# What the planner of a TensorE-bound kernel counts: instruction fetches, and the SBUF turns of VectorE and GpSimd

## The chip, the cores and the metric

The kernel runs on one core of one Trainium2 chip. The core has five engines that run in parallel, each through its own list of instructions: TensorE (matrix products, PE in the profile, with its weight loads as PEld), VectorE (DVE), ScalarE (ACT), GpSimd (POOL) and SyncE (SP), which issues every DMA of this kernel. [...] The metric is the time of one execution on the device in microseconds (us); lower is better. The median of three runs stands for a kernel.

## The reference

Two computations, one after the other. First a chunked attention: 4 batches of 8 heads, 768 tokens, 64 values per head; every chunk of 32 queries sees 16 tokens to its left, itself, 8 to its right, and 8 memory tokens, so 64 keys. Then a mixture of 8 experts over all 3072 tokens of width 512, with a gate that is balanced by eight rounds of row and column division:

```python
scores = scale * np.matmul(q_c, k_full.transpose(0, 1, 3, 2))
a = np.exp(scores - np.max(scores, axis=-1, keepdims=True))
a = a / (np.sum(a, axis=-1, keepdims=True) + 1e-09)
out[:, :, c_start:c_end] = np.matmul(a, v_full)
...
P = np.exp(logits - logits.max())
for _ in range(8):
    P /= P.sum(1, keepdims=True) + 1e-09
    P /= P.sum(0, keepdims=True) + 1e-09
    P *= N / E
for e in range(E):
    h = np.maximum(x @ w1[e], 0.0)
    out += P[:, e:e + 1] * (h @ w2[e])
```

All of it is float32.

## The kernel before

**The work.** The tokens are cut into six units of 512 tokens. With 8 experts that makes 48 pairs of an expert and a unit, handled in one long sequence. A float32 product is made of float16 products: each operand is split into a high and a low half, and three passes (high by high, and the two mixed ones) are added up in PSUM (`PASSES`, L1625). The products of a unit are made by a scheme with seven block products in place of eight (`P1` to `P7`), so sums and differences of blocks are formed first, by VectorE and GpSimd, and split too. A product task on TensorE (`product`, L1629) is 6 or 12 matmuls of 256 columns; the first expert's second layer (`plain_output`, L2138) has tasks of 6 matmuls of 512 columns.

**The attention** is done in 24 blocks of 128 queries (`transposed`, `scores`, `values`), between the products of the first five units. A block has four short tasks of four 128x128 transposes (`tq`, `tk`, `tx`, `ta`) and two bursts: the scores (`sp`, L1103) and the weighted values (`xp`, L1181), each of 64 small matmuls, every one with a weight load of its own. For each unit of 512 tokens come 32 small matmuls of the gate (`lp`, L1437). The results are turned, scaled and split into the unit's operand `x` (`build`, L1283), part of which VectorE and GpSimd form (`sums`, L1314). While a bank of PSUM is free and TensorE would wait, `Plan.pad` (L128) puts matmuls on nothing there (`warm`, L428); this stops when the attention's buffers are given back (`turn`, L2253, at the fifth unit).

**The order of work.** The whole kernel is first written down as some thousands of tasks, and `Plan.run` (L139) then puts them into an order by simulating the engines: each task has an engine, a cost in us, a priority (a due time), the tasks that it depends on, and perhaps a PSUM bank that it takes or frees. At each step the task that can start first is issued; among those that can start at once on an engine, the one with the lowest priority value. Only this order goes to the chip: the instructions of an engine are emitted in it, and the framework adds the semaphore waits that the data need. The costs and the simulated times have no other effect. DMA tasks follow a simple model of one pipe (`pipe`, L143): a transfer starts behind those before it, and the issuer may run up to `BEHIND` = 5 us ahead.

Details that matter here:

- The products of one sequence are chained (`last_pe`, L1646), so among themselves they stay in one order; what the planner decides on TensorE is where attention tasks, the gate, small reductions and `plain_output` go between them.
- Tasks that read PSUM or free something urgently have a priority 200 us ahead of time (`FIRM`).
- In the steady stage (from the fifth unit on, `LATE`) a unit is 28 product tasks of the first layer and 14 of the second; VectorE does, among others, `c` (L1695, one input from PSUM), `ss` (L1794), `h` (L1838 and L1854), `acc` (L1969, L2003); GpSimd does `acc` (L1959), and the sums of blocks of the weights (`ws`, L620).
- `first_hidden` (L2049) makes the first layer of the first unit in two groups g of 256 tokens, each in two steps k. Its tokens come from `xops[0][0]`, apart from g = 1, k = 0, whose tokens lie in a corner of another buffer (`room`, L2058). `xops[0][1]` is the list of the four splits that make them, in the order (g, k) = (0,0), (0,1), (1,1), (1,0) (`build`, L1371 to L1380). The task for (g, k) depends on entry 2g + k (L2085).
- `burst` and `quiet` (L163, L196) could keep two bursts apart by `APART`, which is 0.

## Time and profile before

| what | us |
|---|---|
| median of 3 runs | 1923.76 (1922.41 to 1924.03) |
| the profiled execution, its own time | 1923.72 |
| its span, first to last instruction | 1921.9 |
| TensorE busy in the span | 1893.2 |
| VectorE, ScalarE, GpSimd busy | 1461.6, 1026.7, 545.8 |

The profile is one execution. It lists groups of instructions by line, engine and tile, who waited for whom, the chain of work that ended last, the busy time of each engine in any stretch, and the DMA queues. A matmul row counts matmuls; each has a weight load beside it, listed as PEld. "Busy" of TensorE is not the same as fast: the profile also lists the clock that TensorE was granted (PEclk). "Issue" is waiting for which the profile shows no other engine or transfer as the cause.

### The profile page before, as it was taken

Reading aid. Unit: us, or ns where it says so; the run is one execution under the profiler, and the core shown is the slowest. Engines: PE = TensorE matmul, PEld = TensorE weight load, DVE = VectorE, ACT = ScalarE, POOL = GpSimd, SP = SyncE. Lnnn points to the kernel's source line nnn. Section 1 sums busy time; section 2 is a strip of 40 time slices with the busy share of each in tenths; the row PEclk is TensorE's granted clock in tenths of the full one; section 3 lists DMA queues with packets and bytes.
Section 4 is the critical chain, followed back from the end, with each engine's and each line's share of the span. In section 5 each row is a group of like instructions: output and inputs, shape, how many; then the busy total and the mean of one; then the engine's idle time right before and its main releaser. Section 6 shows DMA issues by size and latency. Waiting matters only on the chain.

```text
span 1921.9 us, 46741 instructions
## 1 busy us (share of the span) xinstructions
PE 1893.2 (99%) x19467; PEld 1628.2 (85%) x19467; DVE 1461.6 (76%) x2417; ACT 1026.7 (53%) x2008; POOL 545.8 (28%) x576
## 2 busy tenths in 40 slices
PE   8899999999999999999999999999999999999999
PEld 7666676688888888888888888888888888888888
DVE  5876879778679866898668875898678885786565
ACT  6665554656456545646445554655555564564453
POOL 2421102434223321442124231342124232332112
PEclk9999999999999999999999999999999999999999
DMA  9866863453234342255215433244413632322321
GB/s 214 205 131 148 222 178 120 135 180 136 84 121 160 127 145 87 89 192 180 91 62 171 175 105 127 89 159 163 140 45 122 222 124 91 102 84 83 127 83 67
DMA packets 209100, 253.98 MB, mean 132 GB/s; under 512 B 108792, under 2 KB 142584, under 8 KB 204536
## 3 DMA queue, kind: packets, MB, share of 16 engines
q1 hardware_dynamic: 208888, 251.00, 41.8%
q8 instruction: 152, 2.49, 0.5%
q14 instruction: 60, 0.49, 0.1%
HBM read 187.51 MB, written 63.44 MB: 131 GB/s over the span
## 4 chain that ended last, share of the span: by engine, by line
PE 92%; DVE 5%; DMA 1%; issue 1%; ACT 1%; SPq 0%; POOL 0%; DVEq 0%; POOLq 0%; ACTq 0%
PE px L1636 25%; PE yx L1636 23%; PE pz L1636 12%; PE yz L1636 11%; PE py L1636 6%; PE yy L1636 6%; PE yp L2154 4%; DVE ss L1794 1%; PE xp L1181 1%; PE pp L2073 1%; PE sp L1103 1%; DVE x L523 1%; PE warm L428 1%; PE ta L1170 1%; PE tq L1040 0%
## 5 line engine op out<-in xcount | busy, mean ns | idle before, releaser
L1636 PEld LDWEIGHTS <-w 128*128 128x128 f16 x7896 | 771.3, 98 | 99.0 <-issue 8.0
L1636 PEld LDWEIGHTS <-h 128*128 128x128 f16 x7056 | 690.4, 98 | 80.9 <-issue 1.1
L1636 PE MATMUL px<-x,w 128*128 128x256 f16 x4512 | 549.6, 273 | 5.5 <-DVE c L1695 3.4
L1959 POOL TENSOR_TENSOR acc<-acc,y 128x256 f32<-128x256 f32 x252 | 269.5, 1076 | 881.7 <-ACT y L1934 868.4
L1636 PE MATMUL yx<-w,h 128*128 128x256 f16 x4032 | 467.5, 273 | 0.7 <-ACT y L1934 0.7
L1685 ACT ACTIVATE q<-px 128x256 f32<-128x256 f32 x376 | 143.1, 382 | 299.2 <-PE px L1636 295.1
L1636 PE MATMUL pz<-x,w 128*128 128x256 f16 x2256 | 278.2, 273 | 0.7 <-DVE c L1695 0.7
L1636 PE MATMUL yz<-w,h 128*128 128x256 f16 x2016 | 233.8, 273 | 0.0
L1854 DVE TENSOR_TENSOR h<-ss,h 128x1024 f16<-128x1024 f32 x160 | 208.6, 1305 | 3.9 <-ACT h L1830 3.7
L1805 ACT ACTIVATE h<-c 128x768 f16<-128x768 f32 x168 | 140.8, 838 | 110.4 <-DVE c L1695 110.4
L1830 ACT CAST h<-ss 128x1024 f16<-128x1024 f32 x168 | 174.2, 1039 | 30.2 <-DVE ss L1794 30.1
L1838 DVE SCALAR_TENSOR_TENSOR h<-c,h 128x768 f16<-128x768 f32 x168 | 167.5, 997 | 12.8 <-ACT h L1805 12.5
L1794 DVE SCALAR_TENSOR_TENSOR ss<-c,ss 128x256 f32<-128x256 f32 x336 | 168.7, 502 | 8.1
L1695 DVE SCALAR_TENSOR_TENSOR c<-px,q 128x256 f32<-128x256 f32 x188 | 78.6, 421 | 107.0 <-PE px L1636 101.6
L1636 PE MATMUL py<-x,w 128*128 128x256 f16 x1128 | 139.5, 273 | 0.0
L1934 ACT ACTIVATE y<-yx,pscale 128x256 f32<-128x256 f32 x168 | 79.4, 474 | 112.5 <-PE yx L1636 108.5
L2154 PE MATMUL yp<-w,h 128*128 128x512 f16 x576 | 131.1, 379 | 0.1
L1794 DVE SCALAR_TENSOR_TENSOR ss<-c,h 128x512 f32<-128x512 f32 x168 | 125.9, 749 | 2.5 <-ACT h L1782 2.5
L1695 DVE SCALAR_TENSOR_TENSOR c<-py,q 128x256 f32<-128x256 f32 x188 | 78.8, 422 | 60.3 <-PE py L1636 54.5
L1636 PE MATMUL yy<-w,h 128*128 128x256 f16 x1008 | 116.9, 273 | 0.0
L2154 PEld LDWEIGHTS <-h 128*128 128x128 f16 x576 | 55.1, 98 | 61.9 <-issue 1.8
L515 ACT ACTIVATE w<-ws,sw 128x1024 f16<-128x1024 f32 (+1 forms) x64 | 69.5, 1088 | 60.5 <-POOL ws L620 60.5
(168 smaller groups left out, 1783.2 us busy)
## 6 DMA issues: line engine op xcount, KB each, us to landing
x<-xkeep SPq DMA_DIRECT2D x28, 1792.0 KB
akeep<-acc SPq DMA_DIRECT2D x168, 256.0 KB
acc<-akeep SPq DMA_DIRECT2D x168, 256.0 KB
w1f<-in_moe_w_dram SPq DMA_DIRECT2D x36, 512.0 KB
w2f<-in_moe_w_dram SPq DMA_DIRECT2D x32, 512.0 KB
w1fm<-in_moe_w_dram SPq DMA_DIRECT2D x28, 512.0 KB
w2fm<-in_moe_w_dram SPq DMA_DIRECT2D x28, 512.0 KB
xkeep<-x SPq DMA_DIRECT2D x6, 1792.0 KB
```

The lines of the kernel that those rows point to most:

```text
L515: lambda: nc.scalar.activation(dst(0), src(), AF.Copy, scale=s),
L1636: nc.tensor.matmul(dst.t, a, b, start=(not more and n == 0), stop=(n == end), skip_group_check=more,)
L1685: lambda: nc.scalar.activation(t.t, src.t, AF.Copy, scale=DOWN),
L1695: lambda: nc.vector.scalar_tensor_tensor(c.t[:, o], src.t, DOWN, q.t, op0=ALU.mult, op1=ALU.add),
L1794: lambda: nc.vector.scalar_tensor_tensor(dst(), src(), 0.0, other(), op0=ALU.max, op1=op),
L1805: lambda: nc.scalar.activation(h.t[:, 0, 0:3], c.t, AF.Relu),
L1830: lambda: nc.scalar.copy(h.t[:, 0, 3:7], ss.t),
L1838: lambda: nc.vector.scalar_tensor_tensor(h.t[:, 1, 0:3].rearrange("p a n -> p (a n)"), c.t.rearrange("p a n -> p (a n)"), 0.0, h.t[:, 0, 0 ...
L1854: lambda: spare.tensor_tensor(h.t[:, 1, 3:7], ss.t, h.t[:, 0, 3:7], op=ALU.subtract),
L1934: (lambda: nc.scalar.activation(t.t, src.t, AF.Copy, scale=f))
L1959: lambda: nc.gpsimd.tensor_tensor(acc.t[:, cols], acc.t[:, cols], q.t, op=ALU.add),
L2154: nc.tensor.matmul(py.t, hf.t[:, hl, where[fh], o : o + P], room(fp, WIDE * wl + DM * fh, WIDE * wl + DM * (fh + 1)), start=(fp == 0 and i ...
```

## The change

The planner's model gets two more things, and many costs in it are corrected. No instruction is added to the kernel or taken out of it, apart from the number of padding matmuls, which `pad` works out from the simulated gaps; the instructions come in another order.

**Fetches.** Every TensorE task gets a `size`, its number of instructions (two per matmul: weight load and product; two passes for a float32 one). `count` adds them up. Whenever the count passes 161 + 256k, a fetch is noted, taken to land 1.4 us later plus 0.8 of the backlog of the DMA pipe, at most 6 us; instructions behind number 449 + 256k can't start before it has landed. `earliest` gives the time at which a task can start so that it doesn't run into a fetch that hasn't landed, and `run` uses it as one more condition of the start. `burst`, `quiet` and `late` are gone.

**Turns on SBUF.** Tasks of GpSimd (but the partition reduction) and those of VectorE that are marked `port=True` are simulated as taking turns: such a task starts no earlier than 0.3 us before the end of the other engine's last one. Their costs become those of the operation by itself (GpSimd's 128x256 operation 0.74 in place of 0.9 or 0.95, and so on).

**One dependency.** The task for (g, k) in `first_hidden` depends on entry 3g + k - 2gk, that is 0, 1, 3, 2 for (0,0), (0,1), (1,0), (1,1).

```diff
-APART = 0.0
+BLOCK = 256
+ASKS = 161
+HELD = 288
+FETCH = 1.4
+QUEUED = 6.0
+FREE = 0.3
...
+        t.size = size
+        t.port = eng == "POOL" if port is None else port
...
                     self.fill(bank, n)
                     heappush(banks, (now + 0.11 * n + 0.2, bank))
+                    self.count(2 * n, now, 0.11 * n)
...
+    def count(self, size, at, cost):
+        while self.counted + size > self.asks:
+            when = at + cost * (self.asks - self.counted) / size
+            queued = min(0.8 * max(self.pipe - when, 0.0), QUEUED)
+            self.fetches.append((self.asks + HELD, when + FETCH + queued))
+            self.asks += BLOCK
+        self.counted += size
+        self.fetches = [f for f in self.fetches if f[1] > at + cost]
+
+    def earliest(self, t, at):
+        for end, landed in self.fetches:
+            if t.size and self.counted + t.size > end:
+                at = max(at, landed - t.cost * (end - self.counted) / t.size)
+        return at
...
-                        if t.burst and at < quiet:
-                            late = (at, t, a) if late is None else late
-                            continue
+                        at = self.earliest(t, at)
                         if pick is None or at < pick[0]:
                             pick = (at, t, a)
...
             t.start = at
-            if t.burst:
-                quiet = at + APART
+            if t.size:
+                self.count(t.size, at, t.cost)
+            if t.port:
+                at = max(at, self.held["POOL" if t.eng == "DVE" else "DVE"] - FREE)
+                self.held[t.eng] = at + t.cost
...
-            sums.append(add("POOL", 0.95, tt(*op), [ld] + sums[-1:], prio - 5, [st, ws]))
+            sums.append(add("POOL", 0.74, tt(*op), [ld] + sums[-1:], prio - 5, [st, ws]))
...
             takes=sp,
-            burst=True,
+            size=4 * H * CB,
...
-        t = add("PE", 0.9, go, [t] + lv, at + 2, [vt, aT], takes=xp, burst=True)
+        t = add("PE", 0.9, go, [t] + lv, at + 2, [vt, aT], takes=xp, size=4 * H * CB)
...
-        t = add("PE", cost, go, list(deps) + [last_pe[0]], now[0], bufs, takes=takes)
+        t = add("PE", cost, go, list(deps) + [last_pe[0]], now[0], bufs, takes=takes, size=int(24 * cost / STEP / 2))
...
             "POOL" if aside else "DVE",
-            2.3 if aside else 1.23,
+            2.15 if aside else 1.23,
             lambda: spare.tensor_tensor(h.t[:, 1, 3:7], ss.t, h.t[:, 0, 3:7], op=ALU.subtract),
             [shi],
             at - 1.0,
             [h, ss],
+            port=True,
...
-                    [t, *wmade, xops[0][1][2 * g + k]],
+                    [t, *wmade, xops[0][1][3 * g + k - 2 * g * k]],
```

## The prediction, made before the result was known

> **What bounds the kernel now.** I read the page first, then the busy time by stages, who TensorE waited for after the first 50 us, and the chain of work that ended last.

> ```profile
> span 1921.9 us, 46741 instructions
> ...
> PE 1893.2 (99%) x19467; PEld 1628.2 (85%) x19467; DVE 1461.6 (76%) x2417; ACT 1026.7 (53%) x2008; POOL 545.8 (28%) x576
> ...
> q8 instruction: 152, 2.49, 0.5%
> ```

> ```profile
> 0.00:50.00 50.00, 43.47 (x789) 35.24 (x790) 30.38 (x63) 31.04 (x63) 14.06 (x25) 0.97 0.98 210
> 50.00:355.00 305.00, 292.17 (x4521) 207.69 (x4519) 240.88 (x447) 169.99 (x342) 66.51 (x77) 0.99 0.65 164
> 355.00:420.00 65.00, 61.26 (x464) 45.11 (x462) 51.98 (x67) 32.98 (x61) 35.24 (x32) 1.00 0.51 171
> 420.00:1900.00 1480.00, 1477.52 (x13530) 1323.56 (x13529) 1133.98 (x1834) 789.85 (x1538) 425.62 (x436) 1.00 0.36 121
> ```

> TensorE is the bound: busy in 1893.2 of 1921.9 us. The second fence is the busy time by stages (columns: length, then PE, PEld, DVE, ACT, POOL; the granted clock; DMA share; GB/s). From 420 to 1900 us TensorE is idle for 1480 - 1477.52 = 2.48 us at full clock: three quarters of the kernel have almost nothing to give. The idle time is in the attention: 305 - 292.17 = 12.83 us from 50 to 355, 3.74 in the next 65, and 6.53 in the first 50, where the DMA share is 0.98.

> ```profile
> PE sp L1103 <- issue: 5.2, 3, 2.2
> PE px L1636 <- ACT q L1685: 2.1, 2, 1.7
> ...
> PE lp L1437 <- issue: 1.5, 1, 1.5
> ```

> ```profile
> 21.96 2.47 issue
> ...
> 44.43 7.00 DMA k<-in_k_dram
> ...
> 86.01 2.23 issue
> ...
> 121.37 1.60 issue
> ...
> 168.36 1.33 issue
> ...
> 237.66 1.52 issue
> ```

> Half of the 12.83 us is put down to nothing ("issue"): three waits in the score bursts and one in the gate's. All four stand in the chain that ended last (start, length, what), so each delays the end: 2.23 + 1.60 + 1.33 + 1.52 = **6.68 us**. A fifth, 2.47, comes before 50 us, and behind it the chain runs through a 7.00 us DMA.

> **What the four are.** The same table by stages, cut at these stalls, counts the matmuls between them:

> ```profile
> 32.00:88.20 56.20, 49.17 (x1014) 36.97 (x1014) 46.82 (x76) 40.09 (x80) 18.34 (x18) 1.00 0.93 219
> 88.20:122.95 34.75, 31.58 (x507) 21.75 (x506) 27.77 (x46) 20.36 (x42) 11.80 (x16) 0.95 0.64 146
> 122.95:169.65 46.70, 44.58 (x759) 31.14 (x760) 32.35 (x56) 26.03 (x52) 6.42 (x9) 1.00 0.61 131
> 169.65:239.10 69.45, 67.74 (x1264) 47.89 (x1264) 53.61 (x89) 35.55 (x76) 7.16 (x9) 1.00 0.80 192
> ```

> With a weight load each they are 2028, 1014, 1518 and 2528 instructions, just short of 8, 4, 6 and 10 blocks of 256 (2048, 1024, 1536, 2560). The page's queue for instructions moved 2.49 MB in 152 packets, and 2 x 19467 / 152 = 256. So TensorE runs out of instructions at a block's boundary, when the next block is late. Why it is late, the DMA queues show, from 81.05 to 87.0 us:

> ```profile
> q1 hardware_dynamic: 705, 2.18, 94.6%
> q8 instruction: 1, 0.02, 1.0%
> ```

> and the busy time in the five us before the stall:

> ```profile
> 81.05:86.00 4.95, 4.92 (x146) 4.01 (x144) 4.57 (x9) 3.78 (x9) 0.00 (x0) 1.00 0.98 383
> ```

> The DMA engines are full there (0.98), and one block's packet is among 706. Meanwhile 146 matmuls, 292 instructions, went by: two bursts and short tasks. The same number in products of six matmuls in 0.66 us would take 16 us. A block is late where bursts follow each other while the queue is full.

> **The change part by part.**

> *The fetch model.* `earliest` holds back a burst that would run into a block still on its way; a task of 12 instructions goes first. That costs nothing where such a task is ready, and behind each of the four stalls one was run at once. The most to be had is 6.68 us and one clock loss:

> ```profile
> 88.20:92.80 4.60, 4.55 (x41) 3.24 (x48) 1.98 (x3) 1.76 (x4) 1.37 (x3) 0.63 0.43 94
> ```

> ```profile
> 89.06 1.49 PE L2073 MATMUL pp<-x,w 128*128 128x256 f16 x6
> ...
> 92.72 0.89 PE L1181 MATMUL xp<-v_pair,at 64*32 64x65 f32 x64
> 93.54 0.83 PE L2073 MATMUL pp<-w,w 128*128 128x256 f16 x6
> ...
> 95.52 0.82 PE L2073 MATMUL pp<-x,w 128*128 128x256 f16 x6
> ```

> After the 2.23 us stall the granted clock was 0.63 for 4.6 us. Three tasks of six matmuls took from 89.06 to 92.72, 3.66 us; the next three took from 93.54 to 95.52, 1.98. That is 1.68 us more, so 8.36 in all. After the three shorter stalls the clock stayed at 1.00. [...]

> Against it stands how the planner counts. Between the stalls 20, 10, 18 and 32 instructions are missing to whole blocks: TensorE issues things that are no matmul and no weight load (waits, it seems), and `size` has no term for them. The planner's boundary then lies behind the real one by at least 20, 30, 48 and 80 instructions at the four stalls, up to a third of a block. The early two should be foreseen; for the later two, I take half. Bounds: all 8.36, or the first stall alone (2.23 + 1.68 = 3.91).

> *What is late next.* A burst held back gives its scores later, and VectorE's work behind them. The nearest row for a product that waits for VectorE in this stage is the first here:

> ```profile
> 137.25 0.81 PE L1636 MATMUL pz<-x,w 128*128 128x256 f16 x6 [0.73 <-DVE c L1695]
> ...
> 842.77 0.82 PE L1636 MATMUL px<-x,w 128*128 128x256 f16 x6 [0.62 <-DVE c L1695]
> ...
> 1505.35 0.81 PE L1636 MATMUL px<-x,w 128*128 128x256 f16 x6 [0.62 <-DVE c L1695]
> ```

> I take one such wait, +0.73; bounds 0 and two.

> *The first 50 us.* A stall of 2.47 could go, but the DMA share there is 0.98 and the planner has little but padding to run meanwhile. I take 0; bounds 0 and -2.47.

> *Turns on SBUF.* The rows bear the rule out:

> ```profile
> 363.76 2.89 POOL L1854 TENSOR_TENSOR h<-ss,h 128x1024 f16<-128x1024 f32 x1 [2.64 <-ACT h L1830]
> 364.60 2.61 DVE L1794 SCALAR_TENSOR_TENSOR ss<-c,h 128x512 f32<-128x512 f32 x1
> ...
> 407.62 0.68 DVE L1794 SCALAR_TENSOR_TENSOR ss<-c,h 128x512 f32<-128x512 f32 x1
> ...
> 1903.12 0.73 POOL L1959 TENSOR_TENSOR acc<-acc,y 128x256 f32<-128x256 f32 x1 [8.68 <-DMA acc<-akeep]
> ```

> VectorE's sum takes 0.68 us alone and 2.61 when GpSimd has begun (364.60 + 2.61 = 367.21, just 0.56 behind GpSimd's end at 366.65). GpSimd's 0.73 agrees with the new 0.74. On the chip nothing changes but the order: simulated VectorE becomes later, so other tasks are ready when it picks. What it can win are the waits for VectorE and ScalarE after 355 us, 3.74 + 2.48 = 6.22; products keep their order there, and VectorE is busy 1133.98 of 1480, so it has room. What it can lose is the last rival. The sign is open; I take 0, bounds -6.22 and +9.9 (below). SyncE issues the same DMAs in an order that follows the tasks; at a DMA share of 0.36 to 0.65 after 50 us I take nothing for it.

> *The dependency.*

> ```profile
> 62.08 1.21 DVE L523 SCALAR_TENSOR_TENSOR w<-xg,sx,w 128x512 f16<-128x512 f32 x1
> ...
> 70.59 0.82 PE L2073 MATMUL pp<-w,w 128*128 128x256 f16 x6
> ```

> The tokens in the corner are ready at 63.29, and the first product that reads them starts at 70.59 without a wait: seven us of cover, so 0. Without the cover it would cost one split, 1.21.

> **The sum.** Profiled execution 1923.72 (span 1921.9 and 1.8 around it; the median, 1923.76, is 0.04 more): -2.23 - 1.68 - 1.60 for the early two, -(1.33 + 1.52)/2 = -1.43 for the later two, +0.73. That is -6.21: **1917.5 us**. Its own range: 1915.4 (all 8.36, nothing back) to 1921.3 (3.91 won, two waits of 0.73 back).

> **Rivals.**

> 1. *The stalls only move.* The miscount of 20 to 80 instructions puts the planner's boundaries beside the real ones; bursts are spaced where it doesn't matter, and as many blocks are late elsewhere. For it: the miscount. Against: the first stalls lie where it is small. Time 1923.7, give or take two waits of 1.3. The same time comes if "issue" isn't a late block at all. [...]

> 2. *More goes than the stalls.* With true times of VectorE the waits after 355 us go as well: 1923.72 - 8.36 - 6.22 = 1909.1. For it: `c` (L1695), for which TensorE waits, queues behind VectorE's blocked sums. Against: product order is fixed, and those waits name ScalarE and DMAs too.

> 3. *Slower: VectorE's new order makes TensorE wait in the steady stage.* Today the 0.62 us wait comes once per expert: the rows at 842.77 and 1505.35 are the first and last of four, 220.9 us apart, so a unit is 36.8 us and the stage has 40. If a sum goes ahead of `c` in every second unit, 20 waits in place of 4 cost 16 x 0.62 = 9.9, and with the 6.2 won: 1927.4. It decides from ten further waits on. For it: the order repeats with each expert, so one bad place is paid many times. Against: `c` has a priority 200 us ahead.

> **How the numbers follow.** Forecast 0.50, rival 1 0.25 (0.02 of it for the deep store), rival 2 0.15, rival 3 0.10. The range reaches from 1909 to 1926: it leaves out most of rival 3 and the lower half of rival 2, 0.15 together. About 0.2% (3.85 us) is what a measurement can tell here, so faster means below 1919.9: 0.43 of the forecast, all of rival 2, 0.02 of rival 1: 0.60. Slower: 0.08 of rival 3 and 0.02 of rival 1: 0.10. The same: 0.30.

> **What would show it.** The new profile should have fewer and shorter "issue" waits of TensorE between 50 and 250 us, the early ones gone first; no stretch of clock 0.63 near 90 us; products between bursts where the DMA share is high; the steady stage still idle for 2 to 3 us. As many "issue" waits as before speaks for rival 1, a steady stage idle for over 8 us for rival 3. A new wait of several us for VectorE or a DMA in the attention would make the sum wrong though its steps be right.

## The result, and the profile after

The change makes the kernel faster by more than twice what was forecast.

| | before | after |
|---|---|---|
| median, us | 1923.09 (1921.62 to 1924.03, 4 runs) | 1908.78 (1905.76 to 1909.61, 4 runs) |
| ratio | | 0.9923, 95% interval 0.9906 to 0.9941 |
| time of the profiled execution | 1923.72 | 1905.76 |
| its span | 1921.9 | 1904.0 |

The profiled execution of after is the quickest of its four. A second profile of the same kernel (e5 below) took 1908.40, close to the median; where a size matters, both stand.

From the page of after, its span and the busy times:

```profile
span 1904.0 us, 46736 instructions
...
PE 1889.6 (99%) x19471; PEld 1626.9 (85%) x19471; DVE 1455.4 (76%) x2417; ACT 1028.3 (54%) x2008; POOL 536.6 (28%) x576
```

The busy time of after by the four stages, in the columns of the prediction's second fence:

```profile
0.00:50.00 50.00, 43.54 (x850) 34.74 (x850) 30.94 (x62) 30.32 (x61) 14.06 (x25) 0.97 1.02 209
50.00:355.00 305.00, 300.27 (x4530) 213.53 (x4529) 247.79 (x462) 178.22 (x354) 70.53 (x84) 1.00 0.66 167
355.00:420.00 65.00, 64.90 (x531) 51.77 (x530) 45.99 (x70) 36.19 (x70) 31.09 (x27) 1.00 0.60 202
420.00:1900.00 1480.00, 1480.00 (x13560) 1326.33 (x13558) 1130.17 (x1825) 783.59 (x1524) 420.96 (x441) 1.00 0.36 121
```

TensorE's idle time fell from 1921.9 - 1893.2 = 28.7 us to 1904.0 - 1889.6 = 14.4, its busy time by 3.6. Look at the last row first: 1480.00 of 1480, where before had 1477.52. TensorE does not wait in the steady stage any more, and from 355 to 420 us it waits 0.10 in place of 3.74. That is 6.12 us which the forecast put at nothing. Who TensorE waited for from 355 to 1900 us in before (line, whom it waited for: us in all, times, longest); the same list of after is empty:

```profile
PE px L1636 <- DVE c L1695: 3.4, 5, 0.9
PE px L1636 <- ACT q L1685: 2.1, 2, 1.7
PE yx L1636 <- ACT y L1934: 0.7, 1, 0.7
```

In the attention (second row) the idle time went from 12.83 to 4.73. Who TensorE waited for there, first the rows of before that the prediction didn't need:

```profile
PE sp L1103 <- DVE xq L1202: 1.6, 1, 1.6
...
PE sp L1103 <- ACT kC L1061: 1.2, 1, 1.2
PE tk L1044 <- DMA k<-in_k_dram: 1.2, 1, 1.2
PE xp L1181 <- DVE s L1123: 1.0, 1, 1.0
```

and the whole list of after:

```profile
PE sp L1134 <- issue: 1.2, 1, 1.2
PE pp L2117 <- issue: 0.8, 2, 0.5
PE xp L1212 <- DVE s L1154: 0.7, 1, 0.7
PE lp L1472 <- DMA gate<-in_moe_w_gate_dram: 0.7, 1, 0.7
PE tk L1075 <- DMA k<-in_k_dram: 0.7, 1, 0.7
PE tq L1071 <- DMA q<-in_q_dram: 0.6, 1, 0.6
```

The waits put down to "issue" went from 6.68 to 2.0 us (1.2 + 0.8), and the others from 12.83 - 6.68 = 6.15 to 4.73 - 2.0 = 2.73. The two largest of the others (scores that wait for VectorE's `xq` and for ScalarE's `kC`) are gone. No stretch near 90 us has a low clock any more.

So the 17.9 us between the two spans are: 4.7 of waits put down to "issue", 3.4 other waits in the attention, 6.1 waits after 355 us, 1.68 of clock, and about 2 of busy time that I did not follow further. Two landmarks cut the span in two for the experiments: the first of the eight column sums of the balancing (`cp`), where the attention is over, and the last group of 24 products. In the timeline of TensorE (start, length, line, operation), first before, then after:

```profile
293.91 0.28 PE L1572 MATMUL cp<-cs,one 128*128 128x8 f32 x2
...
1916.03 2.78 PE L1636 MATMUL yx<-w,h 128*128 128x256 f16 x24
```

```profile
283.35 0.28 PE L1610 MATMUL cp<-cs,one 128*128 128x8 f32 x2
...
1898.08 2.78 PE L1676 MATMUL yx<-w,h 128*128 128x256 f16 x24
```

To the first landmark after is 10.56 us ahead; from it to the second it takes 1614.73 in place of 1622.12, another 7.39. Padding aside, as many matmuls lie before the first landmark in before as in after. Below, "attention" is the first landmark's time and "the rest" the distance between the two.

### The profile page after: what moved, and what is told of

Its sections match the earlier page's. It is cut to its first block, busy times and chain, and to the rows that moved or that the text cites. A ratio compares the mean times of both kernels' runs of the same rounds, so it can differ in the third digit from the quotient of the medians.

```text
span 1904.0 us, 46736 instructions
## 1 busy us (share of the span) xinstructions
PE 1889.6 (99%) x19471; PEld 1626.9 (85%) x19471; DVE 1455.4 (76%) x2417; ACT 1028.3 (54%) x2008; POOL 536.6 (28%) x576
## 3 DMA queue, kind: packets, MB, share of 16 engines
q8 instruction: 152, 2.49, 0.6%
## 4 chain that ended last, share of the span: by engine, by line
PE 95%; DMA 2%; DVE 2%; issue 0%; ACT 0%; SPq 0%; POOL 0%; ACTq 0%; POOLq 0%; DVEq 0%
PE px L1676 25%; PE yx L1676 23%; PE pz L1676 13%; PE yz L1676 12%; PE py L1676 6%; PE yy L1676 6%; PE yp L2200 5%; PE pp L2117 1%; PE xp L1212 1%; PE sp L1134 1%; PE ta L1201 1%; DMA w1fm<-in_moe_w_dram 0%; PE tk L1075 0%; DMA w1f<-in_moe_w_dram 0%; PE tq L1071 0%; DVE x L553 0%
## 5 line engine op out<-in xcount | busy, mean ns | idle before, releaser
L2003 POOL TENSOR_TENSOR acc<-acc,y 128x256 f32<-128x256 f32 x252 | 265.0, 1059 | 872.6 <-ACT y L1978 860.1
```

The lines of the kernel that those rows point to most:

```text
L2003: lambda: nc.gpsimd.tensor_tensor(acc.t[:, cols], acc.t[:, cols], q.t, op=ALU.add),
```

## Experiments

My theory after the result: the turns on SBUF take away the waits after 355 us, and the fetch model the stalls in the attention. The rivals: the fetch model alone does most of it; or the new order is a lucky one, and any change of order would give another time. All kernels below are after with the edit shown, and do the same work; only the order and the amount of padding differ. Each ratio is to before on the same chip, with its 95% interval. Medians are subtracted only between runs of one chip, e1 to e4, e5 to e8, e9 to e12, and e13 to e16; before took 1924.74, 1924.25, 1923.85 and 1925.49 us on these four. The columns from "attention" on are of one profiled execution each.

| run | median us | ratio | attention | the rest | idle after 355 | "issue", 50 to 420 | padding |
|---|---|---|---|---|---|---|---|
| before | 1923.09 | | 293.91 | 1622.12 | 6.22 | 6.7 | 115 |
| after | 1908.78 | 0.9923 | 283.35 | 1614.73 | 0.10 | 2.0 | 119 |
| e1 no turns | 1920.07 | 0.9974 (0.9961 to 0.9987) | 289.97 | 1624.44 | 5.36 | 1.0 | 114 |
| e2 no fetch model | 1909.88 | 0.9916 (0.9900 to 0.9931) | 288.30 | 1615.88 | 0.42 | 3.1 | 125 |
| e3 neither | 1927.54 | 1.0016 (1.0005 to 1.0026) | 294.78 | 1625.71 | 5.69 | 5.3 | 116 |
| e4 before's costs, with the fetch model | 1915.59 | 0.9947 (0.9932 to 0.9962) | 285.63 | 1621.04 | 5.31 | 3.5 | 116 |
| e5 after again | 1908.40 | 0.9924 (0.9912 to 0.9937) | 284.95 | 1615.77 | 0.65 | 2.5 | 119 |
| e6 as e2 | 1908.83 | 0.9922 (0.9908 to 0.9935) | 285.50 | 1615.63 | 0.34 | 1.7 | 125 |
| e7 boundary 128 earlier | 1915.27 | 0.9957 (0.9945 to 0.9970) | 289.82 | 1617.22 | 0 | 0.6 | 138 |
| e8 count 1.2% larger | 1920.18 | 0.9981 (0.9969 to 0.9992) | 295.69 | 1618.27 | 0 | 5.5 | 163 |
| e9 turns only late | 1909.56 | 0.9925 (0.9910 to 0.9941) | 286.47 | 1614.58 | 0 | 1.4 | 114 |
| e10 turns only early | 1917.78 | 0.9965 (0.9952 to 0.9978) | 282.94 | 1625.17 | 6.06 | 0.3 | 119 |
| e11 turns of the wrong ones | 1928.13 | 1.0024 (1.0014 to 1.0034) | 294.48 | 1625.20 | 3.70 | 0.5 | 206 |
| e12 one cost 10 ns larger | 1907.12 | 0.9909 (0.9893 to 0.9925) | 284.23 | 1615.58 | 0 | 2.1 | 119 |
| e13 e4, boundary 128 earlier | 1914.95 | 0.9948 (0.9930 to 0.9966) | 285.64 | 1625.48 | 7.55 | 1.2 | 124 |
| e14 e4, count 1.2% larger | 1917.93 | 0.9969 (0.9956 to 0.9983) | 291.24 | 1622.24 | 4.57 | 2.5 | 138 |
| e15 boundary 64 earlier | 1917.56 | 0.9964 (0.9949 to 0.9979) | 289.21 | 1620.06 | 0 | 1.2 | 154 |
| e16 boundary 64 later | 1910.01 | 0.9924 (0.9907 to 0.9941) | 284.71 | 1614.46 | 0 | 1.9 | 140 |

"Idle after 355" is the length less TensorE's busy time from 355 to 1900 us, "issue" the sum of such waits of TensorE from 50 to 420, and "padding" the number of matmuls on nothing.

**Which part it is: e1 to e4.** e1 takes the turns out, e2 the fetch model:

```diff
-        t.port = eng == "POOL" if port is None else port
+        t.port = False
```

> The changed kernel without the turns of VectorE and GpSimd in the simulation (the fetch model and the new costs stay). Theory A, the fetch model alone made the gain: within 2 us of the changed kernel's 1908.8, TensorE idle under 0.5 us from 420 to 1900 us and under 0.5 from 355 to 420. Theory B, the waits after 355 us went because of the turns: 1915, idle from 420 to 1900 back at about 2.5 us and from 355 to 420 at about 3.7. Theory C, any new order loses or finds such waits by chance: neither 0 nor 6.2 but something else after 355 us.

```diff
-            if t.size and self.counted + t.size > end:
+            if False:
```

> The changed kernel with a fetch that never holds a task back (turns and new costs stay). Theory A: the 'issue' waits of TensorE between 50 and 250 us come back, four to seven of them with 5 to 8 us together, and the time is 1914 to 1918. Theory B: besides that the stage after 355 us stays without idle time (under 0.5 us), so the loss is the stalls alone. Theory C: the idle time after 355 us changes too.

e3 has both edits, so that only the new costs and the new dependency are left.

> Only the new costs and the dependency; neither fetches nor turns. Theory A: as e2, 1914 to 1918. Theory B, turns: 1920 to 1923, with the stalls and with 2.5 us idle from 420 to 1900 us. If the corrected costs took the late waits away: 1914 to 1918 with under 0.5 us idle after 355 us.

e4 has the first edit, and all costs as they were before; so before with the fetch model and the dependency. Of its edit:

```diff
-            sums.append(add("POOL", 0.74, tt(*op), [ld] + sums[-1:], prio - 5, [st, ws]))
+            sums.append(add("POOL", 0.95, tt(*op), [ld] + sums[-1:], prio - 5, [st, ws]))
...
-            2.15 if aside else 1.23,
+            2.3 if aside else 1.23,
```

> The fetch model and the dependency, with the old costs and no turns. Theory A: 1909 to 1913. Theory B (true times of VectorE): the stalls go, but 355 to 420 us and 420 to 1900 us keep about 3.7 and 2.5 us of idle time: 1914 to 1917.

These four ran on one chip, where before took 1924.74. The new costs alone are slower than before by 0.05 to 0.26%. On top of them the fetch model gains 1927.54 - 1920.07 = 7.5 us, the turns 1927.54 - 1909.88 = 17.7. The two don't add up: both together (after, e5) have the ratio of the turns alone. On before's costs the fetch model gains 1924.74 - 1915.59 = 9.2 us by itself. So the gain of the whole change comes with the turns, and beside them the fetch model is worth nothing that can be measured. That went against my theory, by which the stalls had to come back in e2 and cost their time: they came back by 1 us only (3.1 against 2.0).

Where e1 loses, its waits after 355 us show:

```profile
PE px L1676 <- ACT q L1725: 2.1, 2, 1.5
PE px L1676 <- DVE c L1735: 1.3, 5, 0.4
PE yx L1676 <- DVE acc L2013: 1.1, 2, 0.6
PE yx L1676 <- ACT y L1978: 0.6, 1, 0.6
```

It is the kind of list that before has. The rest takes 1624.44 us in e1 and 1625.71 in e3, 2.3 and 3.6 longer than in before. The new costs of GpSimd are true for an operation by itself, and smaller (0.74 for 0.95): in before's trace 36 of its 252 additions to `acc` ran while VectorE did nothing and took 0.72 to 0.73 us, the other 216 took 0.72 to 1.72. Without turns nothing in the model stands for that difference any more. That this is why the late stages are slower than with the old, too large costs is my reading; no run changes GpSimd's costs alone.

**Again, and where the boundary lies: e5 to e8.** e5 is after, unchanged, and e6 is e2, unchanged.

> The changed kernel itself once more, beside the next three on one chip. 1907 to 1911 if the kernel before is at 1923 to 1925.

> e2 once more, so that it stands beside the changed kernel. If the fetch model is worth nothing once the turns are in: within 1.5 us of e5. If it is worth the 4.9 us that separate the two profiles at the first column sum of the gate (283.35 and 288.30): 4 to 6 us above e5.

e7 puts the planner's boundaries half a block before where they are in after; e8 makes its count grow faster, as if the waits that TensorE's queue carries besides matmuls and weight loads were counted.

```diff
-ASKS = 161
+ASKS = 33
```

> The changed kernel with its block boundaries laid half a block wrong (first fetch at count 33 in place of 161). If it matters that the planner knows where the blocks end: more 'issue' waits after 50 us than the changed kernel's 1.95 us, 4 us or more, and 2 to 6 us above e5. If holding bursts apart anywhere does it, or the fetch model does nothing here: within 1.5 us of e5.

```diff
-        self.counted += size
+        self.counted += size * 1.012
```

> The changed kernel with a count that runs 1.2% faster, for the instructions that are neither matmul nor weight load. If that miscount is what leaves stalls: under 1 us of 'issue' waits after 50 us in place of 1.95, and 1 to 2 us below e5. If not: within 1.5 us of e5, with no fewer waits.

e5 and e6 agree within 0.02% of ratio, each with an interval of about 0.13% to either side: beside the turns these runs show no effect of the fetch model on the time. e8 is the miss of this study. I had taken the missing 20 to 80 instructions for the weak point of the change. (Counted from the start in before's trace, 34 to 94 are missing at the four stalls; 1.2% of the count there is 36 to 96.) With a count nearer to the real one the kernel should have stalled less and been quicker. It is 12 us slower than e5, and its issue waits are 5.5 us. From its timeline:

```profile
81.36 0.85 PE L1134 MATMUL sp<-kC,qT 64*32 64x64 f32 x64
82.14 0.28 PE L455 MATMUL warm<-ident 128*128 128x256 bf16 x1
82.92 2.36 PE L455 MATMUL warm<-ident 128*128 128x256 bf16 x20 [0.50 <-issue]
```

The planner holds a burst back, finds nothing else and pads: 21 matmuls on nothing from 82.14 to 85.28, and a stall of 0.50 among them all the same. In all e8 pads with 163 matmuls and after with 119 (groups by line: count, shortest/median/longest in ns, first and last start):

```profile
L455 PE MATMUL warm<-ident x163: 269/273/421, 1.6 to 290.8; 128*128 128x256 bf16 x163
```

```profile
L455 PE MATMUL warm<-ident x119: 270/273/422, 1.6 to 107.6; 128*128 128x256 bf16 x119
```

Of the 10.7 us by which e8 reaches the first landmark later than e5, 8.7 are busy time of TensorE (281.05 against 272.38), with 44 more matmuls of padding, and 2.1 idle time.

e7 has the fewest issue waits of the four, 0.6, and is 6.9 us slower than e5. Two of its waits are longer, from the list of 0 to 420 us:

```profile
PE lp L1472 <- DMA gate<-in_moe_w_gate_dram: 3.8, 1, 3.8
PE cp L1610 <- DVE cs L1582: 3.2, 2, 2.9
```

The gate's matmuls wait for their DMA, and the last column sums for VectorE, with no other work left to lay beside them; in e5 the column sums wait 0.2 us in all, in after not at all. But these waits are not most of the loss: to the first landmark TensorE is idle for 1.0 us less in e7 than in e5 and busy for 5.9 us more, with 19 more matmuls of padding at 0.27 us each. The 3 us wait at the column sums comes behind the landmark. The time in "issue" does not tell which order is quick. By profile, e7 has 1.4 us fewer of it than after and is 9 us longer.

**Where the turns work: e9 to e12.** The padding function is there during the attention and taken away after it, so one condition lets the turns work late only (e9) or early only (e10):

```diff
-            if t.port:
+            if t.port and self.fill is None:
```

> The changed kernel with turns simulated only from the point at which the attention's buffers are given back. Theory B (turns give the planner VectorE's true times, and that removes the late waits): TensorE idle from 355 to 1900 us under 1 us in place of e1's 5.4, so about 5 us below e1: 1914 to 1916. The attention stage as in e1 (first column sum of the gate near 290 us in the profile).

```diff
-            if t.port:
+            if t.port and self.fill is not None:
```

> The same with turns only up to that point. Theory B: idle from 355 to 1900 us at 4 to 6 us, as in e1; the first column sum of the gate near 284 us, as in the changed kernel; 1913 to 1915. If late waits come from the state in which the attention leaves VectorE: idle under 1 us.

e11 makes VectorE take turns for the wrong operations: for those without the mark (most read PSUM) instead of those with it.

```diff
-        t.port = eng == "POOL" if port is None else port
+        t.port = eng == "POOL" or (eng == "DVE" and not port)
```

> The changed kernel with the marks on VectorE turned round: the operations that take turns on the chip are simulated as free, and those that don't (PSUM readers above all) as taking turns. Theory B: 4 us or more of idle time between 355 and 1900 us, and 1914 to 1925. Theory C (any delay of VectorE in the simulation does it): under 1 us of it, 1907 to 1911.

e12 changes one cost of VectorE by 10 ns, to see whether after has a lucky order.

```diff
-        return add("DVE", 1.21, go, deps, prio, [st])
+        return add("DVE", 1.22, go, deps, prio, [st])
```

> The changed kernel with one cost 10 ns longer (VectorE's maximum of a weight block, 1.22 for 1.21), which means nothing on the chip but gives TensorE another order in the attention. If the attention's time follows from the model: within 2 us of the changed kernel, 1906 to 1911. If it hangs on the chance of each order: 3 to 10 us away, in the attention stage alone, with the idle time from 355 to 1900 us still under 1 us.

e9 has all of after's time, e10 does not. Busy time of TensorE from 355 to 420 and from 420 to 1900 us (length, busy, clock, DMA share, GB/s), first of e10, then of e9:

```profile
355.00:420.00 65.00, 62.99 (x502) 1.00 0.51 175
420.00:1900.00 1480.00, 1475.95 (x13507) 1.00 0.36 121
```

```profile
355.00:420.00 65.00, 65.00 (x519) 1.00 0.58 186
420.00:1900.00 1480.00, 1480.00 (x13560) 1.00 0.36 121
```

e10 waits 6.06 us there and e9 not at all. e9 and e1 have the same order on TensorE up to the first column sum and differ behind it only; the rest takes 1614.58 in the one and 1624.44 in the other. Of these 9.9 us, 7.3 are idle time and 2.6 busy time of the same matmuls; the ratios are 0.49% apart, some 9.4 us. This settles the late part: the turns, simulated after the attention, take it from 1624 to 1615. And it is the order on the other engines that does it, VectorE's above all: after and e10 have the same order on TensorE up to the first column sum and differ behind it by the place of 10 matmuls, but 277 of VectorE's 2,417 instructions stand elsewhere, and 105 of ScalarE's 2,002. (Such counts are of the built kernels' instruction lists: how many have to be moved at least to turn one order into the other, padding aside.)

The table says the same of all runs. With turns simulated late for the right operations (after, e2, e5 to e9, e12, e15, e16) the idle time after 355 is 0 to 0.65 us; without (before, e1, e3, e4, e10, e13, e14) it is 4.57 to 7.55.

The idle times came close to what theory B has (6.06 in e10 for 4 to 6, 3.70 in e11 for 4 or more); the times did not. e9 is 4 us quicker than was expected, e10 and e11 are 3 us slower.

e11 is slower than before: the rest takes 1625.20, and its first two waits from 280 to 1900 us are

```profile
PE cp L1610 <- DVE cs L1582: 3.3, 2, 3.0
PE px L1676 <- DVE c L1735: 2.2, 4, 1.0
```

The first lies before 355 us, and e7, e8 and e15 have it too; the second is of the kind that the turns took away. So it is not that a slower VectorE in the model does good; the right operations must be held. In the attention e11 also has 87 more matmuls of padding than after, so its whole time tells less than its idle time after 355. In before's trace the two kinds differ too. VectorE's sum with two inputs in SBUF (`ss`, 128x512) takes 0.68 to 0.69 us in the 111 cases in which GpSimd does nothing meanwhile, and 1.21 to 2.61 in the 11 in which GpSimd works for over 95% of it (the other 46 took 0.67 to 1.22). `c`, which reads PSUM, takes 0.38 to 0.43 us in 457 cases of the first sort and 0.41 to 0.43 in 73 of the second. e11 against after agrees with that as a choice of what the planner should hold. And not all waiting is at a semaphore: the sum of 2.61 us in the prediction, 0.68 alone, reads as one that waited for GpSimd within its own time.

e12's order is little different: 55 of TensorE's 17,702 matmuls stand elsewhere, all in the attention, and 18 of VectorE's instructions. Its time is the same (1907.12). By itself that says little of a lucky order. In e2, e9 and e16 413 to 450 of the matmuls stand elsewhere than in after, and their ratios are after's within the intervals; with the idle times after 355 above, a lucky order falls for the late part. For the attention it stays open (see e7, e8 and e15).

What the turns change on VectorE is seen at the place of the 0.62 us wait which the prediction showed at 842.77, once per expert. The timeline of VectorE in before:

```profile
840.11 0.41 DVE L1695 SCALAR_TENSOR_TENSOR c<-px,q 128x256 f32<-128x256 f32 x1
840.45 0.61 DVE L1794 SCALAR_TENSOR_TENSOR ss<-c,ss 128x256 f32<-128x256 f32 x1
840.98 0.41 DVE L1695 SCALAR_TENSOR_TENSOR c<-pz,q 128x256 f32<-128x256 f32 x1
841.32 0.61 DVE L1794 SCALAR_TENSOR_TENSOR ss<-c,ss 128x256 f32<-128x256 f32 x1
841.96 0.42 DVE L1695 SCALAR_TENSOR_TENSOR c<-py,q 128x256 f32<-128x256 f32 x1
842.30 0.41 DVE L1695 SCALAR_TENSOR_TENSOR c<-px,q 128x256 f32<-128x256 f32 x1
```

and the same place in after:

```profile
825.12 0.41 DVE L1735 SCALAR_TENSOR_TENSOR c<-px,q 128x256 f32<-128x256 f32 x1
825.45 0.61 DVE L1835 SCALAR_TENSOR_TENSOR ss<-c,ss 128x256 f32<-128x256 f32 x1
826.10 0.42 DVE L1735 SCALAR_TENSOR_TENSOR c<-py,q 128x256 f32<-128x256 f32 x1
826.44 0.41 DVE L1735 SCALAR_TENSOR_TENSOR c<-px,q 128x256 f32<-128x256 f32 x1
826.77 0.74 DVE L1735 SCALAR_TENSOR_TENSOR c<-pz,q 128x256 f32<-128x256 f32 x2
```

In before one more `ss` (0.61) and a `c` of `pz` stand between the first and the second `c` of `px`, which frees the bank that TensorE waits for; in after the `pz` comes behind it. The second starts 2.19 us after the first in before, 1.32 in after, and the product on TensorE goes on without a wait:

```profile
826.50 1.47 PE L1676 MATMUL px<-x,w 128*128 128x256 f16 x12
```

**The boundary once more, without and with turns: e13 to e16.** e13 and e14 are e4 with the edits of e7 and e8; e15 and e16 are after with the boundary 64 instructions earlier and later.

> The kernel of e4 (fetch model on the old costs, no turns) with its boundaries half a block wrong. If e4 gains because its bursts are held where the real block ends: the gain of 9 us mostly goes, 1920 to 1925, with 5 us or more of 'issue' waits after 50 us. If any holding apart of bursts does it, or the chance of another order: 1912 to 1919.

> The kernel of e4 with the count that runs 1.2% faster, so that its boundaries lie where the chip has them. If the place of the boundaries matters: fewer 'issue' waits after 50 us than e4, and 1911 to 1915. If holding itself costs time where nothing else is ready (as the padding in e8 suggests): more padding than e4's 116 matmuls, and slower than e4 in spite of no more 'issue' waits.

```diff
-ASKS = 161
+ASKS = 97
```

> The changed kernel with its boundaries 64 instructions earlier, about where the missing instructions put the real ones at 170 us. If the place of the boundaries matters beside turns: at or below the changed kernel, 1905 to 1908. If the attention's time is chance or cost of holding: 1909 to 1920, with no link to the 'issue' waits.

```diff
-ASKS = 161
+ASKS = 225
```

> The same, 64 instructions later, away from the real ones. If the place matters: more 'issue' waits than the changed kernel and 1910 to 1915. Otherwise 1907 to 1920 with no such link.

A boundary that is wrong by half a block gains as much without turns as the right one (e13 0.9948, e4 0.9947), and e14, with a count nearer to the real one, gains less. e16 equals after within its interval. e15 is slower: like e7 it has more padding and the 3 us wait at the column sums. Without turns the fetch model does take "issue" waits away (5.3 us in e3, 1.0 in e1), but its gain in time does not come from knowing where the blocks end. e13 has few issue waits (1.2) although its boundaries are wrong, and keeps the late waits (7.55).

What no run varies is how long the model takes a fetch to last, at most 1.4 + 6.0 us. In the trace of e8 the block that TensorE needed before it could go on at 122.27 was due to be asked for at 114.06 (by the number of instructions at which blocks are asked for, last section); its packet began at 119.76 and took 0.88 us. From the asking to the going on that is 8.2 us, more than the model allows. So a count that is nearly right need not prevent the stall; whether a longer fetch in the model would, was not tried.

What makes one order end the attention at 283 to 287 us and another at 288 to 296 is not settled. Part of it is seen (new waits for the gate's DMA, padding), and part is the execution: e1 and e9, with the same order there, end it at 289.97 and 286.47, e2 and e6, the same kernel, at 288.30 and 285.50. In both pairs the later one has more busy time for the same matmuls up to the landmark (275.04 against 272.32, 276.55 against 272.89) and a lower granted clock (0.98 against 0.99, 0.98 against 1.00). The old dependency together with the new model wasn't tried.

## Why the prediction was wrong, point by point

1917.5 us was forecast, 1909 to 1926 as the range; 1908.78 came, 14.3 us less than before in place of 6.2. Rival 2 (1909.1, with a chance of 0.15) had the late part for the right reason. That its time fits so well is in part luck: it took all 8.36 us of stalls and clock as won, where 6.4 were, and the other waits in the attention, which it does not name, made up for that.

- **What bounds the kernel**: right. TensorE is still the bound, 99% busy.
- **Turns on SBUF, "the sign is open; I take 0"**: the step that failed most. Measured: 6.1 us of idle time after 355 in the profiles of before and after, 5.6 with e5, all of the 6.22 in e9 and e12. I had named the 6.22 as what could be won, had the 2.61 against 0.68 us to show that the old costs were wrong where it mattered, and weighed a threat (rival 3) against it for which no row spoke. The argument against rival 2, that the order of products is fixed, was no argument: it is the order on the other engines, VectorE's above all, that sets these waits (e10 against after). Rival 3 has its mechanism in the new costs without the turns, where the rest grew by 2.3 to 3.6 us (e1, e3), but not in the change.
- **"What is late next", +0.73**: wrong in sign. The other waits in the attention fell from 6.15 to 2.73 us, 2.89 in e5. The planner with turns orders VectorE's and GpSimd's work there too, and I had followed the turns only behind 355 us. That the turns made these waits fall is not shown. With the new costs, TensorE is idle from 50 to 355 us for 3.6 to 6.4 us in all in seven runs where the attention is planned with turns (after, e2, e5, e6, e10, e12, e16), and for 7.3 to 15.5 where it isn't (e1, e3, e9); but with turns and the boundary moved in e7, e8 and e15 it is 8.7 to 13.2. And on the old costs, without turns, the other waits fell to 3.3 us as well (e4, e13). The cause of this term stays open.
- **The stalls, -5.26 of 6.68**: right in size (-4.7; -4.2 in e5), and not for the reason given. Which stalls go came in part the other way round: the early ones were to go and the later ones to be halved, but in after the one near 88 us stays (1.19) and those near 123, 170 and 239 are gone; e5 keeps 1.66 at 89.27 and 0.82 at 162.34. Without the fetch model they fall nearly as far once the turns are in (3.1 and 1.7 left in e2 and e6), and with boundaries that are wrong by half a block they fall as well (e7, e13). That the later two stalls would be met by halves, because the count is 20 to 80 instructions short, has no support: with a fuller count the kernels are slower (e8, e14).
- **The clock, -1.68**: came as forecast in after. No 0.63 near 90 us. e5 still has a stall there, of 1.7 us, and keeps the full clock behind it, but its clock falls elsewhere: to 0.50 from 54 to 56 us, behind a wait of 2.25 us for a DMA. So the stretch near 90 went, but where the low clock falls changes from one execution to the next. The waits of e5 from 50 to 355 us and its busy time behind the stall:

```profile
PE sp L1134 <- issue: 2.5, 2, 1.7
PE tk L1075 <- DMA k<-in_k_dram: 2.2, 1, 2.2
PE xp L1212 <- DVE s L1154: 0.8, 1, 0.8
```

```profile
89.00:94.00 5.00, 4.74 (x131) 4.09 (x131) 3.88 (x7) 1.65 (x4) 0.91 (x2) 1.00 0.38 84
```

- **The first 50 us, 0**: right in sum (idle 6.53 before, 6.46 after), by luck: the stall of 2.47 us shrank to 0.96, and a new wait of 2.09 for ScalarE's `w` came at 31.19.
- **The dependency, 0**: right. Put into before alone it changes no engine's order of instructions, so it is worth exactly nothing there.
- **Rival 1** (the stalls only move) fell: they went. What remains of its doubt is that right boundaries weren't needed for it (e7, e13). No run shows a deep store of instructions, which had 0.02 of its chance; in its place the runs showed "issue" waits at 449 plus whole multiples of 256 instructions, and a block asked for some 288 instructions ahead (last section).

By e5, which ran near the median, the terms are -4.2 stalls, -3.3 other waits in the attention, -5.6 after 355, +0.9 of idle time in the first 50 us and -3.1 of busy time, in which the clock is: -15.3, the whole of the 15.3 us between the two profiled times. The forecast had the stalls and the clock, and of the next two terms, 8.9 us, it had the one at nothing and the other with the wrong sign.

## What to carry to other kernels

A planner's costs must be true together: an operation's lone duration (0.68 us for the sum of the prediction, which also took 2.61 beside GpSimd) is right only if the model also knows whom it has to wait for; here true costs without the turns were slower than before, and with them 17.7 us quicker than that. Where a part of a change is aimed at a few waits that stand in the profile by name, and the new model explains them, a forecast of nothing needs a row that speaks against it; here none did. And an order of several thousand tasks moves as a whole: what a part is worth alone (9.2 us) says little of what it is worth beside another (nothing that could be measured), so take it out of the finished kernel, too, before you keep it.

## What the runs showed of the hardware

The length of one wait does not tell whether the clock falls. A stall of 2.23 us was followed by 4.6 us at 0.63 (before), one of 1.84 by 0.51 and 0.63 in the next two stretches of 2 us (e2, from 90 us), one of 1.7 by none (e5, fence above), and a wait of 2.52 for a DMA by none (e6, at 52.82).

And the same kernel can end the attention 2.8 us apart in two executions (e2 and e6), the same order there 3.5 us (e1 and e9), so one profile of that stage can't tell orders apart that differ by less.
